# New planner costs and a new order for a two-layer attention and MLP kernel

## The chip, the cores and the metric

The kernel runs on one core of one Trainium2 chip. The metric is the device time of one launch in microseconds (us); three runs of the kernel before gave 1412.83 to 1413.08, with a median of 1412.99. The core has five engines that run side by side, each with its own in-order queue: TensorE (PE, matmuls into PSUM), ScalarE (ACT, exponentials and gelu), VectorE (DVE, elementwise work), GpSimd (POOL) and SyncE (SP, which issues DMAs). They wait for one another by semaphores.

## The reference

Four residual blocks: attention, MLP, attention, MLP, both layers with the same weights. S = 2048 rows, D = 512, H = 32 heads of 16 columns, F = 1792.

```python
def _A_ref(x, wqkv, wo):
    qkv = (x @ wqkv).reshape(B, S, 3, H, Dh).transpose(2, 0, 3, 1, 4)
    q, k, v = qkv[0], qkv[1], qkv[2]
    scores = einsum("bhqd,bhkd->bhqk", q, k) * (Dh ** -0.5)
    p = softmax(scores, axis=-1)
    o = einsum("bhqk,bhkd->bhqd", p, v)
    return o.transpose(0, 2, 1, 3).reshape(B, S, D) @ wo

def _B_ref(x, w1, b1, w2, b2):
    return einsum("bsf,fd->bsd", gelu(einsum("bsd,df->bsf", x, w1) + b1), w2) + b2

x = x + _A_ref(layernorm(x), A_wqkv, A_wo)
x = x + _B_ref(layernorm(x), B_w1, B_b1, B_w2, B_b2)
x = x + _A_ref(layernorm(x), A_wqkv, A_wo)
x = x + _B_ref(layernorm(x), B_w1, B_b1, B_w2, B_b2)
```

## The kernel before, in words

**Blocks.** The scores of the two layers are cut into 4096 blocks (called cells in the code) of 128 keys by 512 columns. A block is one matmul on 32 rows of the TensorE array (L1595), so up to four blocks, one for each row group `a` = 0 to 3, run side by side; each fills one PSUM bank. An exponential then turns scores into the weights of the softmax. Most blocks go to ACT: one ACTIVATE (L2245) takes two or three neighbouring banks at once. There are two slots of banks, (0, 1, 2) and (3, 4), and later bank 5 joins the second; while ACT works on one slot, PE fills the other. The other blocks go to DVE, which evicts a bank with one multiply and add into 16-bit integers that are the bits of a rough exponential (L1862, `dfirst`); POOL or DVE adds constants to make shifted copies (L2108 and L2110, `shift`, `dchain`), and their products with V and with three scaled copies of V (`vcopies`, L1523) are summed. So a block on ACT costs PE one product with V (L2312, `pvs`) and a block on DVE four. Four products run side by side in a round on 32 columns each.

**Passes.** `passes` cuts the work into 84 passes, each for one group of heads in one segment of query rows. The table KD lists for each kind of pass the key blocks that DVE may take: 1320 blocks in all. In the order that the kernel before issues, DVE takes 1236 of them. Counted by pass, the missing 84 are: 17 of 32 in the first eight passes, 36 of 160 in the next eight (these 16 are the first segment of layer 0), 4 in the rest of layer 0, 27 in the 25 passes of layer 1 that alternate between its first two segments, and none in the last 19 passes. A listed block that DVE doesn't take goes to ACT (`next_act`).

**Side work.** Layernorm, the projections, the output matrix, the two MLP matmuls and the gelu of other segments are spread between the exponentials. A gelu needs another activation table than the exponential, so each pair of gelu ACTIVATEs (L1273) has a table load before and after it. Where PE would idle long, the planner inserts matmuls whose result isn't used (`fill`, L1583).

**The planner.** The order of every engine's queue is written out when the kernel is built. `_Sched.run` keeps a clock for each engine, looks which operations are ready, and issues the one that can start first; `_ready` adds up when an operation's inputs are there (the end of what makes them, and LATENCY of its engine), `_cost` how long it takes. Priorities decide between operations that are ready, and an operation with a `slack` may be issued ahead of one that would end after it had to start. Before each score matmul, `attach`, `more`, `trade` and `swap` decide whether blocks for DVE, or a third block for ACT, go along: the bank must be free in the plan by the score's start (within TOL or SOFT), and DVE's clock must not be later than SWAP after it. `solo` issues a block for DVE alone when ACT's clock is far ahead of PE's. The costs never reach the chip; there only the order counts, and each engine goes on as soon as its semaphores allow.

The numbers in NAMES are settings of these decisions. ROWS holds sets of them and PIECES says which set is in force in each of 100 equal pieces of the 4096 blocks (`turn`, `take`).

Of the kernel before, what the change touches and what calls it, by code (L numbers as in the profile page):

```python
# [22 lines left out]
PVB = 6  # L23
# [71 lines left out]
         "ALONE", "AHEAD", "PSHIFT", "QUEUE", "SOLO", "BACK", "SIDE", "BOTH", "DMAX", "GMAX", "PMORE", "DUMORE", "GRACE", "PPS", "WAIT", "SOFT",  # L95
         "CLOSE",)
ROWS = (
# [42 lines left out]
)  # L140
PIECES = (5, 12, 11, 14, 27, 2, 39, 7, 26, 39, 20, 29, 23, 24, 15, 13, 24, 19, 11, 24, 24, 37, 25, 40, 37, 16, 30, 36, 38, 2, 21, 15, 39,
          24, 5, 14, 26, 38, 26, 37, 31, 9, 29, 3, 15, 17, 40, 26, 17, 28, 1, 19, 31, 31, 8, 29, 22, 20, 15, 39, 10, 21, 26, 37, 11, 9, 0,
          29, 29, 32, 36, 15, 33, 35, 21, 5, 34, 6, 26, 39, 41, 9, 17, 40, 18, 2, 31, 37, 27, 2, 29, 20, 36, 37, 39, 4, 12, 20, 39, 34)
CLOSE = 0.35
BOTH = 1
DMAX = 2
# [27 lines left out]
RWIDE = 2  # L174
AHEAD = 24
PSHIFT = 3
EXPC = 0.054
PFIX = 0.173
PWORD = 0.00164
VFIX = 0.151  # L180
# [147 lines left out]

OWN = 0.022
HEAD = 0.14  # L330
LATENCY = {"pe": 0.2175, "act": 0.21, "dve": 0.139, "pool": 0.153328, "sp": 0.1}
OVERLAP = 0.083
ROUND = 1.02
MROUND = 1.033


class _Sched:
# [130 lines left out]
    def _cost(self, op):  # L468
        if op.eng == "act" and op.writes[0][0] in "XKQ":
            return 0.48  # L470
        if op.eng == "dve":
            return max(op.cost - OVERLAP, 0.07)
        if op.eng == "pe":
            return op.cost * ((ROUND if op.writes[:1] == ["B.%d" % PVB] else MROUND) if op.mode == "P" else 1.0) + (SW if op.mode != self.mode else 0.0)
        return op.cost

    def active(self, t):
# [106 lines left out]
SW = 0.107  # L584
# [117 lines left out]
class _Plan:  # L702
# [558 lines left out]
    def gelu(self, l, seg):  # L1261
        T = self.T
        n = seg[2]
        for p in range(NFC // 2):
            yield ("need", ("h", l, seg, p))
        half = NFC // GP
# [2 lines left out]
            if n == 512:  # L1269
                g = g.rearrange("p a q -> p (a q)")  # L1270
            gk = self.gkeys(seg, range(f, f + half))
            yield _Op("act", 0.065 + 0.4267 * half * n / 512 + 1.31,
                      lambda e, g=g: e.activation(out=g, in_=g, func=ACT.Gelu_apprx_tanh), reads=gk, writes=gk, prio=2)  # L1273
            for p in range(f // 2, (f + half) // 2):
                yield ("give", ("g", l, seg, p))
# [352 lines left out]
    def turn(self):  # L1628
        self.piece += 1
        globals().update(zip(NAMES, ROWS[PIECES[self.piece]]))  # L1630

    def take(self, c):
        self.scored += 1
        self.left[c[0]] -= 1
        self.due[c[0]] += 1
        if self.piece + 1 < len(PIECES) and self.scored * len(PIECES) >= (self.piece + 1) * self.total:
            self.turn()
# [795 lines left out]
```

## Time and profile before

| what | value |
|---|---|
| median of three runs | 1412.99 us |
| profiled execution, its own time | 1412.66 us |
| profiled execution, span from the first to the last instruction | 1410.8 us |
| mean granted TensorE clock | 1.000 |
| PE busy | 1384.3 us |
| ACT busy | 1387.5 us |
| DVE busy | 1258.0 us |
| POOL busy | 983.4 us |

Busy is the time in which an engine has at least one instruction under way. A group row gives line, engine, operation, tile written and tiles read, the form and the count, then the busy time, the mean duration of one in ns, and the idle time before the group with what ended it. A row of one line's instructions has the shortest, median and longest duration in ns, the first and last start in us, and the most frequent forms of that tile. A timeline row has the start, the length from the first start to the last end, and the count of instructions that were merged; a piece of the chain has start, length and count. A row of a window has its length, then for PE, PE's weight loads, DVE, ACT and POOL the busy time and the count, then the granted clock and the DMA share with GB/s. A row of the waits has who waited for whom, the total in us, how often, and the longest.

### The profile page before, as it was taken

The numbers are of one execution on the slowest core, as the hardware profiler recorded it, in microseconds if no ns is written. First come the engines' busy times: TensorE is split into PE (matmuls) and PEld (weight loads), VectorE is DVE, ScalarE is ACT, GpSimd is POOL, SyncE is SP. The second block draws the span as 40 slices with busy tenths as digits, with TensorE's granted clock in tenths as the row PEclk, the third lists the DMA queues.
The fourth block names the chain that finished last, engine by engine and source line by source line (L and its number), as shares of the span: only waits on it lengthen the run. The fifth ranks groups of instructions, "written<-read, shape, count | busy, mean of one in ns | idle before, by whom it ended". The sixth has DMA issues, their size and how long they took to land.

```text
span 1410.8 us, 45496 instructions
## 1 busy us (share of the span) xinstructions
PE 1384.3 (98%) x19322; PEld 412.1 (29%) x19322; DVE 1258.0 (89%) x2482; ACT 1387.5 (98%) x1398; POOL 983.4 (70%) x1231
## 2 busy tenths in 40 slices
PE   9999999999999999999999999999999999999999
PEld 3222222222222222222222222222222222334346
DVE  8999999988998899988899898899988888999884
ACT  7999999999999999999999999999999999999995
POOL 1479787885877777756775669657876866877671
PEclk9999999999999999999999999999999999999999
DMA  5200000114221232212512241100114223201121
GB/s 148 68 2 2 2 2 18 38 47 128 69 55 31 62 113 69 54 46 86 119 36 50 62 117 58 46 17 17 32 57 116 63 62 117 74 17 40 29 59 55
DMA packets 122307, 80.39 MB, mean 57 GB/s; under 512 B 36732, under 2 KB 121084, under 8 KB 122108
## 3 DMA queue, kind: packets, MB, share of 16 engines
q1 hardware_dynamic: 122108, 77.49, 19.8%
q8 instruction: 155, 2.54, 0.7%
q14 instruction: 44, 0.36, 0.1%
HBM read 65.67 MB, written 4.19 MB: 50 GB/s over the span
## 4 chain that ended last, share of the span: by engine, by line
ACT 90%; PE 8%; DVE 1%; DMA 0%; issue 0%; DVEq 0%
ACT pt L2245 76%; ACT kt L2245 4%; PE ps L712 3%; ACT g L1273 3%; ACT q L2245 3%; ACT v L2245 2%; PE ps L2312 2%; PE ps L1595 2%; ACT L2245 1%; ACT L1273 1%; ACT g L2245 0%; DMA wr<-in_B_w_dram 0%; DVE kt L1862 0%; DVE dp L1862 0%; PE ps L899 0%; DVE stats L845 0%
## 5 line engine op out<-in xcount | busy, mean ns | idle before, releaser
L2245 ACT ACTIVATE pt<-ps 128x1024 bf16<-128x1024 f32 (+1 forms) x1181 | 1173.3, 1219 | 1.3 <-PE ps L1595 1.1
L2108 POOL INT64_ADD dp<-dp x739 | 598.8, 819 | 169.2 <-DVE dp L1862 35.9
L1595 PE MATMUL ps<-qp,kt 32*128 32x512 bf16 x4096 | 540.4, 384 | 12.7 <-ACT pt L2245 8.2
L1862 DVE TENSOR_SCALAR dp<-ps 128x512 uint16<-128x512 f32 x748 | 498.9, 682 | 49.2 <-PE ps L1595 44.3
L1595 PEld LDWEIGHTS ps<-qp,kt 32*128 32x128 bf16 x4096 | 136.0, 91 | 570.1 <-ACT pt L2245 460.4
L2312 PE MATMUL ps<-pt,v 128*17 128x512 bf16 (+1 forms) x2827 | 281.0, 359 | 1.6 <-DVE v L1004 0.7
L2312 PE MATMUL ps<-dp,vc 128*17 128x512 bf16 (+1 forms) x2532 | 279.9, 356 | 0.4 <-ACT pt L2245 0.2
L2108 POOL INT64_ADD kt<-kt x251 | 203.3, 815 | 95.3 <-DVE kt L1862 43.0
L1862 DVE TENSOR_SCALAR kt<-ps 128x512 uint16<-128x512 f32 x256 | 172.3, 683 | 21.5 <-PE ps L1595 19.6
L712 PE MATMUL ps<-xf,wr 128*32 128x512 bf16 (+1 forms) x1888 | 134.1, 365 | 0.0
L2108 POOL INT64_ADD v<-v x119 | 96.7, 817 | 52.4 <-DVE v L1862 16.4
L2312 PE MATMUL ps<-dp,v 128*17 128x512 bf16 (+1 forms) x844 | 123.7, 357 | 3.4 <-DVE xt L1073 2.8
L2312 PE MATMUL ps<-kt,vc 128*17 128x512 bf16 (+1 forms) x954 | 117.7, 339 | 0.9 <-POOL kt L2108 0.6
L712 PE MATMUL ps<-wr,g 128*32 128x512 bf16 x1408 | 106.0, 383 | 0.2 <-DMA wr<-in_B_w_dram 0.2
L2312 PEld LDWEIGHTS ps<-dp,vc 128*17 128x17 bf16 x2532 | 76.5, 89 | 60.5 <-issue 29.0
L1862 DVE TENSOR_SCALAR v<-ps 128x512 uint16<-128x512 f32 x120 | 81.3, 683 | 13.1 <-PE ps L1595 12.1
L2312 PEld LDWEIGHTS ps<-pt,v 128*17 128x17 bf16 x2827 | 70.2, 88 | 75.4 <-issue 54.2
L2108 POOL INT64_ADD xf<-xf x63 | 50.9, 808 | 58.4 <-DVE xf L1862 39.3
L1255 DVE TENSOR_SCALAR g<-ps,hb1t 128x512 bf16<-128x512 f32 (+1 forms) x112 | 78.9, 706 | 6.3 <-PE ps L712 6.2
L2312 PE MATMUL ps<-kt,v 128*17 128x512 bf16 (+1 forms) x449 | 73.8, 352 | 0.3 <-DVE xt L1073 0.2
L2245 ACT ACTIVATE kt<-ps 128x1024 bf16<-128x1024 f32 x64 | 69.0, 1189 | 0.0
L2312 PE MATMUL ps<-v,vc 128*17 128x512 bf16 x360 | 60.4, 381 | 0.1
(127 smaller groups left out, 1450.8 us busy)
## 6 DMA issues: line engine op xcount, KB each, us to landing
wr<-in_B_w_dram SPq DMA_DIRECT2D x174, 256.0 KB, 2.9
wr<-in_A_wqkv_dram SPq DMA_DIRECT2D x24, 256.0 KB, 3.1
x<-in_A_x_dram SPq DMA_DIRECT2D x7, 512.0 KB, 4.6
wr<-in_A_wo_dram SPq DMA_DIRECT2D x10, 256.0 KB, 4.0
kept<-x SPq DMA_DIRECT2D x4, 512.0 KB, 3.0
x<-kept SPq DMA_DIRECT2D x4, 512.0 KB, 3.9
out_dram<-x SPq DMA_DIRECT2D x16, 128.0 KB, 1.7
q<-in_B_w_dram SPq DMA_DIRECT2D x3, 512.0 KB, 5.6
```

The costliest lines, as they stand in the source:

```text
L712: return [lambda e, a=a: e.matmul(out[32 * a:32 * a + 32, :], lhsT=lhsT[:, 32 * a:32 * a + 32], rhs=rhs, start=start, stop=stop, tile_posi ...
L1255: yield _Op("dve", 0.21 + n / 966, lambda e, fc=fc, pb=pb: e.tensor_scalar(T["G"][:, fc, q], pb, T["HB1T"][:, fc:fc + 1], None, op0=ALU.ad ...
L1273: lambda e, g=g: e.activation(out=g, in_=g, func=ACT.Gelu_apprx_tanh), reads=gk, writes=gk, prio=2)
L1595: return (lambda e: e.matmul(o, lhsT=lhsT, rhs=rhs, start=True, stop=True, tile_position=(32 * a, 0)), ["K%d.%d.%d" % (l, gb, kt // 4), "Q ...
L1862: yield _Op("dve", 0.682, lambda e: e.tensor_scalar(u, self.bank(b), E_SCALE, E_BIAS, op0=ALU.mult, op1=ALU.add), reads=["B.%d" % b], writ ...
L2108: op = _Op("pool", PFIX + PWORD * 128 * n * (1 + both), lambda e: e.int64_add(dst, src, by * PACKED), reads=reads, writes=writes)
L2245: yield _Op("act", EXPC + 0.4267 * n, lambda e, src=src, dst=dst: e.activation(out=dst, in_=src, func=ACT.Exp, scale=0.25), reads=["B.%d" ...
L2312: op.fns.append(lambda e, o=o, lhsT=q[0][0][m], rhs=q[0][1][:, n * m:n * m + n], a=a, st=st, sp=sp: e.matmul(o, lhsT=lhsT, rhs=rhs, start= ...
```

## The change

Five numbers of the planner change, one is new, and two are merged:

```diff
-EXPC = 0.054
+EXPC = 0.0635
...
-LATENCY = {"pe": 0.2175, "act": 0.21, "dve": 0.139, "pool": 0.153328, "sp": 0.1}
+LATENCY = {"pe": 0.2175, "act": 0.17, "dve": 0.115, "pool": 0.153328, "sp": 0.1}
 OVERLAP = 0.083
-ROUND = 1.02
-MROUND = 1.033
+ROUND = 1.013
+INTO = 0.008
...
-            return op.cost * ((ROUND if op.writes[:1] == ["B.%d" % PVB] else MROUND) if op.mode == "P" else 1.0) + (SW if op.mode != self.mode else 0.0)
+            return op.cost * (ROUND if op.mode == "P" else 1.0) + (SW + (INTO if op.mode == "P" else 0.0) if op.mode != self.mode else 0.0)
...
-            yield _Op("act", 0.065 + 0.4267 * half * n / 512 + 1.31,
+            yield _Op("act", 0.065 + 0.4267 * half * n / 512 + 1.46,
```

An exponential over n banks costs EXPC + 0.4267 n in the plan. A round of four products or of side work costs `MM` (0.2132) times ROUND, and SW (0.107) is added where PE changes between score matmuls (mode S) and rounds (mode P); INTO comes on top where it changes into rounds.

ROWS has 39 sets in place of 42, and PIECES takes the 39 in a new sequence of 100. The first set and the pieces, before and after (the second number of a set is SLACK, the third LATE, the fifth OPENING):

```diff
-    (0.5, 0.3, 0.7, 0.2, 10, 10, 2, 6, 1, 1, 2, 2, 5, 0.3, 0.4, 2, 3.5, 24, 3, 4, 0.4, 1.0, 0, 1, 2, 3, 1, 2, 0.3, 2, 0.15, 0.0, 0.35,),
...
+    (0.5, 0.1, 0.7, 0.2, 18, 10, 2, 6, 1, 1, 2, 2, 5, 0.3, 0.4, 2, 3.5, 24, 3, 4, 0.4, 1.0, 0, 1, 2, 3, 1, 2, 0.3, 2, 0.15, 0.0, 0.35,),
+    (0.5, 0.3, 0.7, 0.2, 18, 10, 2, 6, 1, 1, 2, 2, 5, 0.3, 0.4, 2, 3.5, 24, 3, 4, 0.4, 1.0, 0, 1, 2, 3, 1, 2, 0.3, 2, 0.15, 0.0, 0.35,),
...
-PIECES = (5, 12, 11, 14, 27, 2, 39, 7, 26, 39, 20, 29, 23, 24, 15, 13, 24, 19, 11, 24, 24, 37, 25, 40, 37, 16, 30, 36, 38, 2, 21, 15, 39,
...
+PIECES = (20, 3, 16, 16, 17, 7, 3, 6, 20, 34, 1, 25, 25, 4, 29, 17, 24, 34, 36, 38, 37, 26, 16, 38, 34, 28, 32, 22, 4, 16, 4, 23, 4, 1, 0,
...
```

Nearly all sets before have SLACK 0.3 and most after have 0.2. Sets of before with MID (the fourteenth number) at 1.4 are gone. KD, the passes, the instructions and their forms are the same.

More of the change, by code (lines that the diff above doesn't have):

```diff
@@ L97 @@
 ROWS = (
[42 rows of a table removed]
-)
-PIECES = (5, 12, 11, 14, 27, 2, 39, 7, 26, 39, 20, 29, 23, 24, 15, 13, 24, 19, 11, 24, 24, 37, 25, 40, 37, 16, 30, 36, 38, 2, 21, 15, 39,
-          24, 5, 14, 26, 38, 26, 37, 31, 9, 29, 3, 15, 17, 40, 26, 17, 28, 1, 19, 31, 31, 8, 29, 22, 20, 15, 39, 10, 21, 26, 37, 11, 9, 0,
-          29, 29, 32, 36, 15, 33, 35, 21, 5, 34, 6, 26, 39, 41, 9, 17, 40, 18, 2, 31, 37, 27, 2, 29, 20, 36, 37, 39, 4, 12, 20, 39, 34)
[39 rows of a table added]
+)
+PIECES = (20, 3, 16, 16, 17, 7, 3, 6, 20, 34, 1, 25, 25, 4, 29, 17, 24, 34, 36, 38, 37, 26, 16, 38, 34, 28, 32, 22, 4, 16, 4, 23, 4, 1, 0,
+          16, 24, 20, 30, 8, 18, 33, 11, 19, 26, 19, 33, 16, 21, 9, 2, 29, 10, 32, 36, 35, 13, 12, 34, 28, 36, 5, 21, 19, 30, 11, 15, 16,
+          38, 25, 30, 5, 26, 24, 29, 3, 28, 16, 27, 23, 30, 0, 22, 15, 24, 23, 30, 21, 33, 11, 14, 24, 30, 10, 31, 16, 36, 38, 8, 4)
 CLOSE = 0.35
```

78 rows, old and new, of the table ROWS are left out of this document.

## The prediction

> **What bounds the kernel now.** I read the page first (busy shares, slices, chain), then one engine at a time: groups by line, single pieces of the chain, three windows, the waits. On the page:
>
> ```profile
> PE 1384.3 (98%) x19322; PEld 412.1 (29%) x19322; DVE 1258.0 (89%) x2482; ACT 1387.5 (98%) x1398; POOL 983.4 (70%) x1231
> ...
> DVE  8999999988998899988899898899988888999884
> ACT  7999999999999999999999999999999999999995
> ...
> PEclk9999999999999999999999999999999999999999
> ...
> ACT 90%; PE 8%; DVE 1%; DMA 0%; issue 0%; DVEq 0%
> ```
>
> Two engines are 98% busy, but the chain that ended last runs over ACT for 90%, and a matmul's recorded end contains its pipeline, so ACT is the candidate. ACT's records overlap too, so "busy" is no proof; the step from one exponential to the next is. Two pieces of the chain, both of exponentials two banks wide:
>
> ```profile
> 451.17 16.50 ACT pt L2245 x18
> 1308.66 6.42 ACT v L2245 x7
> ```
>
> 16.50 / 18 and 6.42 / 7 are both 0.917 us, though one record lasts longer:
>
> ```profile
> L2245 ACT ACTIVATE pt<-ps 128x1024 bf16<-128x1024 f32 x1011 | 970.8, 1158 | 0.2
> L2245 ACT ACTIVATE pt<-ps 128x1536 bf16<-128x1536 f32 x170 | 255.6, 1585 | 1.2 <-PE ps L1595 1.1
> ```
>
> The third bank adds 1585 - 1158 = 427 ns, the planner's 0.4267 a bank. So an exponential costs 0.4267 a bank plus 0.917 - 2 x 0.4267 = 0.0636 fixed: 0.917 for two banks, 1.344 for three. Now the number of each, by the exponentials (first five rows, grouped by the tile written) and the score blocks that VectorE turns into exponentials (last five):
>
> ```profile
> L1595 PE MATMUL ps<-qp,kt 32*128 32x512 bf16 x4096 | 540.4, 384 | 12.7 <-ACT pt L2245 8.2 <-ACT q L2245 0.6 <-ACT v L2245 0.3
> L2245 ACT ACTIVATE pt<-ps x1181: 1018/1178/1756, 12.2 to 1382.0; 128x1024 bf16<-128x1024 f32 x163, 128x1536 bf16<-128x1536 f32 x34
> L2245 ACT ACTIVATE kt<-ps x64: 1018/1179/1642, 200.7 to 836.9; 128x1024 bf16<-128x1024 f32 x61, 128x1536 bf16<-128x1536 f32 x3
> L2245 ACT ACTIVATE v<-ps x49: 1023/1182/1619, 1009.5 to 1380.7; 128x1024 bf16<-128x1024 f32 x43, 128x1536 bf16<-128x1536 f32 x6
> L2245 ACT ACTIVATE q<-ps x37: 1023/1196/1634, 209.0 to 1206.6; 128x1024 bf16<-128x1024 f32 x30, 128x1536 bf16<-128x1536 f32 x7
> L2245 ACT ACTIVATE g<-ps x5: 1024/1208/1720, 875.1 to 902.5; 128x1024 bf16<-128x1024 f32 x3, 128x1536 bf16<-128x1536 f32 x2
> L1862 DVE TENSOR_SCALAR dp<-ps x748: 624/682/693, 33.5 to 1376.8; 128x512 uint16<-128x512 f32 x187
> L1862 DVE TENSOR_SCALAR kt<-ps x256: 627/683/693, 152.5 to 1364.9; 128x512 uint16<-128x512 f32 x128
> L1862 DVE TENSOR_SCALAR v<-ps x120: 629/685/693, 199.9 to 668.0; 128x512 uint16<-128x512 f32 x120
> L1862 DVE TENSOR_SCALAR xf<-ps x64: 645/688/693, 30.4 to 1215.4; 128x512 uint16<-128x512 f32 x64
> L1862 DVE TENSOR_SCALAR xp<-ps x48: 645/682/693, 32.4 to 789.1; 128x512 uint16<-128x512 f32 x48
> ```
>
> Of 4096 blocks, 748 + 256 + 120 + 64 + 48 = 1236 go to VectorE, 2860 to ACT in 1181 + 64 + 49 + 37 + 5 = 1336 exponentials: 2860 - 2 x 1336 = 188 of three banks, 1148 of two. The gelus interrupt them:
>
> ```profile
> 307.27 2.13 ACT L2245 ACTIVATE pt<-ps 128x1024 bf16<-128x1024 f32 x2
> 309.42 1.28 ACT L1273 ACT_TABLE_LOAD   x1
> 310.71 6.27 ACT L1273 ACTIVATE g<-g 128x3584 bf16<-128x3584 bf16 x2
> 317.00 1.28 ACT L2245 ACT_TABLE_LOAD   x1
> 318.29 1.02 ACT L2245 ACTIVATE pt<-ps 128x1024 bf16<-128x1024 f32 x1
> ```
>
> From the end of one exponential (309.40) to that of the next (319.31), less its own 0.917, a gelu pair costs 9.0 us; seven lie between the first and the last exponential (14 of the wide gelus). The sum: 1148 x 0.917 + 188 x 1.344 + 7 x 9.0 = 1368.4, and three casts at the start of some 0.5 make 1369.9. The three windows, before, from first to last exponential, and after (columns PE, PEld, DVE, ACT, POOL):
>
> ```profile
> 0.00:12.23 12.23, 10.46 (x98) 4.63 (x98) 9.74 (x48) 4.89 (x11) 2.87 (x9) 1.00 0.85 250
> 12.23:1383.05 1370.82, 1348.96 (x18613) 391.24 (x18616) 1236.94 (x2394) 1370.16 (x1367) 980.53 (x1222) 1.00 0.20 55
> 1383.05:1410.80 27.75, 24.87 (x620) 16.20 (x612) 11.31 (x41) 12.44 (x21) 0.00 (x0) 1.00 0.17 50
> ```
>
> 1369.9 of 1370.8: ACT stalls for about 1 us in all. So the time is 12.2 (opening) + ACT's work + 27.8 (tail), and an order is worth what it takes off ACT: 2860 blocks x 0.4267 + exponentials x 0.0636. The profiled run took 1412.66 against a span of 1410.8 and a median of 1412.99; I work in the span and add 2.2.
>
> **The change part by part.** No instruction is edited; the planner's numbers and its table of settings change, and the order comes out new.
>
> *Exponential, 0.054 to 0.0635.* The trace says 0.0636. The plan's ACT gets 1336 x 0.0095 = 12.7 us longer, the chip's not at all. *Gelu, 1.31 to 1.46.* Two halves cost 2 x (0.065 + 2.987 + 1.46) = 9.02 in the plan against 9.0 traced (8.72 before): 7 x 0.3 = 2.1 us more plan time. So the plan sees 14.8 us of ACT time that it overlooked, and can fill it with work of the others.
>
> What can move is bounded: the lists KD offer 1320 blocks and 1236 are done, so 84 remain, 53 of them in the first segment's passes (17 in its first eight, 36 in the next eight), 4 later in layer 0 and 27 in the 25 passes of layer 1 in which two segments alternate. Where the list is used up, a slower plan of ACT moves no block. The first 16 passes and those 25 hold 512 + 832 of 4096 blocks, so 14.8 x 1344 / 4096 = 4.9 us of the overlooked time lies there. Back-to-back evictions start 0.60 apart:
>
> ```profile
> 700.04 0.67 DVE L1862 TENSOR_SCALAR kt<-ps 128x512 uint16<-128x512 f32 x1
> 700.64 0.68 DVE L1862 TENSOR_SCALAR dp<-ps 128x512 uint16<-128x512 f32 x1
> ...
> 700.81 0.61 POOL L2108 INT64_ADD kt<-kt  x1 [1.70 <-DVE kt L1862]
> ```
>
> so 4.9 / 0.6 = 8 blocks. Each saves half an exponential, 0.4585: **-3.7 us**. Bounds: all 84, -38.5; and below zero too, since nothing forces a new order to reach 1236: 12 lost (one for each of twelve passes short of blocks, an estimate from the counts above) is +5.5. I take 8 because the rate row is of the very instruction. The cover is VectorE, 1236.94 of 1370.82 busy, and POOL, 980.53; PE pays three more products a block, 3/4 of a 0.213 round, 8 x 0.16 = 1.3 us in its own slack. That slack shows in the waits of score matmuls for a bank, 0.42 each; they come back with more work ahead of them:
>
> ```profile
> PEld ps L1595 <- ACT pt L2245: 460.4, 1094, 1.3
> PEld ps L1595 <- DVE dp L1862: 12.1, 28, 0.5
> ```
>
> [...]
>
> *Releases: ACT 0.21 to 0.17, DVE 0.139 to 0.115.* The lone exponential above ended at 319.31, and the score that waited for it started at
>
> ```profile
> 319.37 0.10 PEld L1595 LDWEIGHTS ps<-qp,kt 32*128 32x128 bf16 x3 [0.55 <-ACT pt L2245]
> ```
>
> 0.06 later; its record outlasts the step by 1.02 - 0.917 = 0.10, so the plan should charge 0.16: 0.17 fits. For DVE the eviction at 700.04 ends 700.71 and POOL starts 0.10 later: 0.77 from its start, while the plan charges 0.599 + 0.115 = 0.714 (0.738 before). So the new figure lies 0.06 below this row, 0.024 further than the old. In an in-order queue that is a short wait, mostly on POOL (30% idle). I charge ACT +0.7 us of new stalls; bounds 0 and +3 (the 28 waits on an eviction above, grown by 0.1 each).
>
> *Single rounds (1.02 and 1.033 to 1.013, and 0.008 a switch).* A side round in its own visit goes from 0.2203 + 0.107 to 0.216 + 0.115, 0.004 dearer; a product pair 0.005 dearer, a side pair equal. Nothing on the chip: 0, with +-1 for what it reorders.
>
> *Settings and pieces.* Mostly SLACK 0.3 to 0.2. They choose how many exponentials get a third bank: 20 more of three banks drop 10 exponentials, 10 x 0.0636 = **-0.6** (bounds -3 and +3, some hundred either way, an estimate from the 188 there are). Opening: 0, with +-1 (its window has DMA busy for 0.85 of the time, and no load changes). Tail: the ending work is 24.87 of 27.75 us on PE, -0.4 with bounds -2 and +2.
>
> Sum: -3.7 - 0.6 - 0.4 + 0.7 = -4.0. Span 1406.8, time **1408.8** (1412.8 - 4.0, between the profiled run and the median). 0.2% is 2.8 us, about what a measurement here tells from no change.
>
> **The rivals.**
>
> *A: nothing to gain.* In three quarters of the passes the list is used up already, and ACT is back to back, so a truer plan has nothing to repair. Blocks within 6 of 1236: 1412.8 +- 2.8. For it: the missing 1 us of stalls. Against: 84 blocks left.
>
> *B: much more.* A third of the 84 is taken, 28 x 0.4585 = 12.8: 1400. For it: VectorE's idle 134 us in the middle window. Against: the passes short of blocks are the loaded ones (slices of DVE at 9 there).
>
> *C: slower, by lost blocks.* A score may take a VectorE block only if VectorE's plan is free within SWAP 0.5 of the score's start. ACT's release is 40 ns earlier in the plan, so the score starts earlier and VectorE looks 40 ns later; a chance missed costs 0.4585. From 7 lost blocks (3.2 us) it is slower; 14 lost, 1419.2. For it: the first segment's full VectorE. Against: 14.8 us more plan time.
>
> *D: slower, by starved exponentials.* DVE's releases are charged below the row by 0.06; each time PE's queue stands at a product whose block is late, the score behind is late. A score has 0.42 us to spare, so it decides only where three or four such errors add up; 4.7 us of stalls eat the gain, 7.5 make it slower; 70 of 0.15 are 10.5: 1412.8 - 4.7 + 10.5 = 1418.6. Against: 1 us of stalls now.
>
> **How the numbers follow.** Forecast band (-2.8 to -9, that is 1404 to 1410): 0.43. B (below 1404): 0.11. A: 0.21. C: 0.17. D: 0.08. Faster 0.43 + 0.11 = 0.54, same 0.21, slower 0.25. The range, 1402 to 1417, leaves out the far half of B and the far part of C; the likeliest case's own is 1404 to 1410.
>
> **What would show it.** The five counts of VectorE evictions sum to about 1244 (C: below 1230; B: above 1260). Exponentials sum to about 1322, some 208 of three banks. ACT's work by the two steps still accounts for the window from first to last exponential to within 2 us (D: not). Opening 12.2 and tail 27 to 28 us unchanged. I am wrong if the eviction count moves and the time does not follow at 0.4585 a block, or if the tail moves by more than 2 us.

## The result, and the profile after

| | before | after |
|---|---|---|
| median of seven runs, us | 1412.99 | 1417.24 |
| lowest to highest, us | 1412.68 to 1413.17 | 1414.65 to 1419.75 |
| profiled execution, span | 1410.8 | 1415.6 |
| mean granted TensorE clock | 1.000 (profiled execution) | 0.999 in three of seven, else 1.000 |

The ratio is 1.003 (95% interval 1.002 to 1.004): the kernel became slower by 0.3%, 4.25 us, where I had forecast 4.2 us less. It also scatters over 5 us in the seven runs, where the kernel before scatters over 0.5. (In the longer series of the experiments below, on three chips, the kernel before itself spreads over 1.8 to 2.8 us, in 15 to 27 runs each.) The profiled execution took 1417.74. Line numbers are three lower than before.

The page of the kernel after, the lines that answer to those of before:

```profile
PE 1379.4 (97%) x19360; PEld 413.4 (29%) x19360; DVE 1259.9 (89%) x2482; ACT 1388.1 (98%) x1377; POOL 994.3 (70%) x1247
...
DVE  8999999889998899988998789999978878999883
ACT  7999999999999999999999999999999999999995
...
PEclk9999999999999999999999999999999999999999
...
PE 56%; ACT 25%; DVE 15%; DMA 2%; POOL 1%; issue 1%; DVEq 0%
```

The busy shares hardly differ from those of before; ACT is again at 98%. The chain that ended last does: ACT carried 90% of it, and now carries 25%, with PE at 56% and DVE at 15%. The shares of the chain overstate what changed, since ACT still works for all but 10 us of the middle, as counted below; but other engines now make it wait at many places.

The counts, by the exponentials of each tile and the blocks that DVE evicts:

```profile
L2242 ACT ACTIVATE pt<-ps x1131: 1018/1081/1685, 12.2 to 1386.8; 128x1024 bf16<-128x1024 f32 x151, 128x1536 bf16<-128x1536 f32 x38
L2242 ACT ACTIVATE v<-ps x67: 1018/1045/1586, 991.4 to 1385.4; 128x1024 bf16<-128x1024 f32 x61, 128x1536 bf16<-128x1536 f32 x6
L2242 ACT ACTIVATE kt<-ps x64: 1018/1070/1557, 201.3 to 830.0; 128x1024 bf16<-128x1024 f32 x53, 128x1536 bf16<-128x1536 f32 x11
L2242 ACT ACTIVATE q<-ps x40: 1018/1079/1602, 224.5 to 1214.3; 128x1024 bf16<-128x1024 f32 x30, 128x1536 bf16<-128x1536 f32 x10
L2242 ACT ACTIVATE g<-ps x13: 1023/1472/1533, 351.5 to 902.8; 128x1536 bf16<-128x1536 f32 x7, 128x1024 bf16<-128x1024 f32 x6
...
L1859 DVE TENSOR_SCALAR dp<-ps x756: 625/680/693, 37.3 to 1381.8; 128x512 uint16<-128x512 f32 x189
L1859 DVE TENSOR_SCALAR kt<-ps x258: 628/682/693, 149.1 to 1373.8; 128x512 uint16<-128x512 f32 x129
L1859 DVE TENSOR_SCALAR v<-ps x110: 650/680/692, 198.5 to 650.5; 128x512 uint16<-128x512 f32 x110
L1859 DVE TENSOR_SCALAR xf<-ps x72: 650/683/692, 29.4 to 1221.7; 128x512 uint16<-128x512 f32 x72
L1859 DVE TENSOR_SCALAR xp<-ps x46: 629/680/692, 31.5 to 789.2; 128x512 uint16<-128x512 f32 x46
```

DVE takes 756 + 258 + 110 + 72 + 46 = 1242 blocks (1236 before), so ACT has 2854, in 1131 + 67 + 64 + 40 + 13 = 1315 exponentials: 2854 - 2 x 1315 = 224 of three banks and 1091 of two. ACT's work is 1091 x 0.917 + 224 x 1.344 + 63.0 for the gelus + 1.5 for the casts = 1366.0, 3.9 us less than before. The three windows:

```profile
0.00:12.23 12.23, 9.19 (x96) 4.26 (x96) 9.74 (x48) 4.89 (x11) 2.88 (x9) 1.00 0.84 248
12.23:1388.22 1375.99, 1346.78 (x18705) 394.23 (x18708) 1240.02 (x2397) 1370.89 (x1346) 991.41 (x1238) 1.00 0.20 56
1388.22:1415.60 27.38, 23.48 (x572) 14.92 (x560) 10.11 (x38) 12.33 (x20) 0.00 (x0) 1.00 0.10 32
```

The opening is the same 12.23, the tail 27.38 for 27.75. The middle holds 1375.99 us for 1366.0 of work: 10.0 us in which ACT stalls, where the kernel before has 1370.82 - 1369.9 = 0.9. So 1410.8 - 3.9 - 0.4 + 9.1 = 1415.6. Nearly all that was to be gained on ACT was gained, and stalls took it twice over.

From here on "stalls" is the sum over all steps from the end of one exponential to the end of the next, less the common step of its width (0.917 and 1.343 us), where that is over 0.012 us: 1.4 us in 16 places before, 10.5 us in 82 places after. The planner's own clock has 1.7 us of ACT idle in the order after and 2.6 in the order before. So before, the chip ran with fewer stalls than planned; after, it has 10.5 - 1.7 = 8.8 us more than its plan.

Some of them name their cause. The waits for DMA in the kernel after:

```profile
PEld ps L709 <- DMA wr<-in_B_w_dram: 4.1, 7, 1.7
PE ps L709 <- DMA wr<-in_B_w_dram: 2.2, 3, 1.4
DVE xln L1325 <- DMA xf<-xln: 1.3, 1, 1.3
DVE xln L873 <- DMA kt<-xln: 1.0, 1, 1.0
```

The second row lies within the first: where PE's weights are late (PEld), its matmuls (PE) are late at the same place. So PE stood for MLP weights for 4.1 us at 7 places; in the kernel before it was this:

```profile
PEld ps L712 <- DMA wr<-in_B_w_dram: 0.8, 2, 0.5
```

One of these stops in the chain (start, length, what), with the exponential behind it:

```profile
1049.38 0.01 PE ps L1592
1049.39 6.69 DMA wr<-in_B_w_dram
1056.08 0.04 issue
1056.12 0.61 PE ps L709 x8
...
1057.11 1.94 ACT L2242 ACTIVATE pt<-ps 128x1024 bf16<-128x1024 f32 x2 [1.13 <-PE ps L1592]
```

An MLP weight load issued at 1049.39 landed 6.69 us later, where the median of the 174 loads of that kind is 3.0. PE's queue stood at the side matmul that needs it, the score behind it was late, and ACT idled for 1.13 us.

### The profile page after: what moved, and what is told of

It reads as the page before. It is cut to its first block, busy times and chain, and to the rows that moved or that the text cites. A ratio compares the mean times of both kernels' runs of the same rounds, so it can differ in the third digit from the quotient of the medians.

```text
span 1415.6 us, 45592 instructions
## 1 busy us (share of the span) xinstructions
PE 1379.4 (97%) x19360; PEld 413.4 (29%) x19360; DVE 1259.9 (89%) x2482; ACT 1388.1 (98%) x1377; POOL 994.3 (70%) x1247
## 4 chain that ended last, share of the span: by engine, by line
PE 56%; ACT 25%; DVE 15%; DMA 2%; POOL 1%; issue 1%; DVEq 0%
ACT pt L2242 20%; PE ps L2309 19%; PE ps L1592 18%; PE ps L709 18%; DVE dp L1859 5%; DVE kt L1859 2%; DMA wr<-in_B_w_dram 1%; ACT v L2242 1%; ACT g L1270 1%; DVE stats L842 1%; ACT q L2242 1%; ACT g L2242 1%; ACT kt L2242 1%; DVE xln L873 1%; POOL dp L2105 1%
## 5 line engine op out<-in xcount | busy, mean ns | idle before, releaser
L2242 ACT ACTIVATE pt<-ps 128x1024 bf16<-128x1024 f32 (+1 forms) x1131 | 1133.5, 1151 | 4.2 <-PE ps L1592 3.3
L2105 POOL INT64_ADD dp<-dp x752 | 607.6, 818 | 167.4 <-DVE dp L1859 39.5
L2105 POOL INT64_ADD kt<-kt x257 | 207.8, 814 | 97.2 <-DVE kt L1859 45.5
L2309 PE MATMUL ps<-pt,v 128*17 128x512 bf16 (+1 forms) x2739 | 266.5, 359 | 1.8 <-POOL kt L2105 0.5
L2309 PE MATMUL ps<-kt,vc 128*17 128x512 bf16 (+1 forms) x960 | 123.1, 339 | 0.7 <-POOL kt L2105 0.4
L2105 POOL INT64_ADD v<-v x110 | 89.7, 821 | 44.7 <-DVE v L1859 19.5
L1859 DVE TENSOR_SCALAR v<-ps 128x512 uint16<-128x512 f32 x110 | 73.7, 681 | 9.0 <-PE ps L1592 8.4
L2242 ACT ACTIVATE kt<-ps 128x1024 bf16<-128x1024 f32 (+1 forms) x64 | 68.5, 1150 | 0.3 <-PE ps L1592 0.2
L2242 ACT ACTIVATE v<-ps 128x1024 bf16<-128x1024 f32 (+1 forms) x67 | 67.2, 1091 | 0.1
```

What stands on the lines that cost most here:

```text
L1859: yield _Op("dve", 0.682, lambda e: e.tensor_scalar(u, self.bank(b), E_SCALE, E_BIAS, op0=ALU.mult, op1=ALU.add), reads=["B.%d" % b], writ ...
L2105: op = _Op("pool", PFIX + PWORD * 128 * n * (1 + both), lambda e: e.int64_add(dst, src, by * PACKED), reads=reads, writes=writes)
L2242: yield _Op("act", EXPC + 0.4267 * n, lambda e, src=src, dst=dst: e.activation(out=dst, in_=src, func=ACT.Exp, scale=0.25), reads=["B.%d" ...
L2309: op.fns.append(lambda e, o=o, lhsT=q[0][0][m], rhs=q[0][1][:, n * m:n * m + n], a=a, st=st, sp=sp: e.matmul(o, lhsT=lhsT, rhs=rhs, start= ...
```

## The experiments

Two theories of the stalls stood at the start. R, the reserve (T in two of the texts below): the old costs had ACT 9.5 ns faster at each exponential than it is, so on the chip ACT fell behind its plan all the time, and whatever came late on PE, DVE, POOL or DMA was made up while it did; the new costs are true, and that reserve is gone. Its rivals: the new releases are too short, or this one order is unlucky. All differences below are between the median of an experiment and that of the kernel before on the same chip.

| run | to before, us | ratio (95%) | stalls, us (places) | runs with clock 0.999 |
|---|---|---|---|---|
| after | +4.25 | 1.003 (1.002 to 1.004) | 10.5 (82) | 3 of 7 |
| new tables, old costs | +31.4 | 1.0223 (1.0204 to 1.0241) | 16.3 (44) | 1 of 2 |
| new costs, old tables | +20.4 | 1.0144 (1.0126 to 1.0163) | 14.7 (69) | 0 of 2 |
| after, small weight loads | +2.21 | 1.0018 (1.0009 to 1.0027) | 7.5 (77) | 5 of 11 |
| the same and three rounds | +1.46 | 1.0009 (1.0001 to 1.0018) | 7.7 (77) | 0 of 11 |
| small loads, small POOL | -0.70 | 0.9996 (0.9986 to 1.0006) | 5.0 (46) | 2 of 8 |
| small loads, small side steps | -1.81 | 0.9988 (0.9978 to 0.9998) | 3.6 (38) | 2 of 8 |
| all four | -2.89 | 0.9978 (0.9968 to 0.9987) | 3.2 (29) | 0 of 9 |
| after, three rounds alone | +2.49 | 1.0017 (1.0007 to 1.0026) | 10.7 (89) | 0 of 10 |
| before, narrow exponentials | -9.78 | 0.9929 (0.9914 to 0.9944) | 6.3 (74) | 0 of 4 |
| before, small side steps | -0.90 | 0.9993 (0.9983 to 1.0003) | 0.7 (9) | 0 of 10 |

**One half of the change alone.** Old costs with the new sets and pieces, and new costs with the old ones (shortened):

```diff
 # e2: the kernel after
-EXPC = 0.0635
+EXPC = 0.054
 # e3: the kernel before
-EXPC = 0.054
+EXPC = 0.0635
 # and LATENCY, ROUND, MROUND / INTO and gelu likewise
```

> The old costs with the new tables of settings. The plan then has 1200 blocks on DVE and 1067 + 254 exponentials, so ACT's work is 14 us longer than before the change, and the plan itself leaves ACT idle for 15 us: about 1436 us by both theories. Theory T (the true costs took away a hidden reserve): unplanned stalls of ACT 1 to 3 us, as before the change. Rival O (this is chance, of one order): 4 to 8 us.

> The new costs with the old tables. The plan has 1218 blocks on DVE, 1131 + 205 exponentials and 10 us of planned idle time of ACT: 1430 us where nothing unplanned comes on top. Theory T (reserve gone): unplanned stalls 6 to 10 us, so 1436 to 1440 us. Rival O (chance of one order): 1 to 4 us, 1431 to 1434 us.

Measured: 1444.71 and 1433.63. Both are far slower than either kernel, with 1200 and 1218 blocks for DVE. Of their stalls the planner's clock has 14.9 and 10.1 us itself. What is not in the plan is 16.3 - 14.9 = 1.4 and 14.7 - 10.1 = 4.6 us by the sums, and 4.2 and about 5 us when it is counted place by place, since some planned stalls don't occur on the chip. For the old costs the first count fits theory T (1 to 3) and the second its rival (4 to 8). For the new costs both counts lie between the two bands, below the 6 to 10 of theory T and above the 1 to 4 of its rival, and the time of 1433.63 is one that the rival had forecast (1431 to 1434). So this pair doesn't decide between the theories, and T missed on the new costs. What it shows is that with either half alone the order gets far worse, so the change can't be priced by undoing a half of it; from here on I kept the orders and changed the work.

The first of them held something else. Windows of 3.4 us in the execution of the old costs with the new tables, with the granted clock third from last:

```profile
487.70:491.10 3.40, 3.16 (x57) 1.29 (x56) 1.90 (x4) 3.38 (x2) 0.91 (x2) 1.00 0.20 41
491.10:494.53 3.43, 1.85 (x30) 0.54 (x26) 1.14 (x2) 3.42 (x4) 0.00 (x0) 1.00 0.87 258
494.53:497.94 3.41, 3.41 (x30) 0.47 (x22) 2.69 (x6) 2.70 (x4) 0.61 (x1) 0.50 0.02 7
497.94:501.35 3.41, 3.41 (x48) 0.95 (x48) 3.09 (x7) 3.25 (x4) 1.41 (x2) 1.00 0.33 86
```

PE waits for most of 491.10 to 494.53; for the next 3.41 us the clock is at half, and ACT, busy before, is busy for 2.70 of 3.41. Counted by the starts of the matmuls (0.213 us for each, the planner's figure, side by side counted once; in this trace seven rounds in a row last 1.69 us and one 0.39, so they follow one another after 0.217), the array works 0.39 of 491.2 to 494.6. In the kernel after, the sparsest such stretch, 0.35, starts at 932.0; in the kernel before it is 0.52. The stretch ahead of the half clock still holds 30 matmuls, and PE's longest wait in it was 1.58 us. That the sparse stretch brought the half clock was my reading of this one place; how sparse the array must be for that, and for how long, was not shown.

**Loads that come in time.** The kernel after, each load of a weight ring slot 32 partitions high instead of 128 from the slot's second use on (the edit is shortened); the order is the same on all engines:

```diff
 def wload(self, piece, src, n, uses, w, over):
-    dst = self.T["WR"][w].rearrange("p (c f) -> p c f", c=n)
+    n = slice(0, 32) if w in self.whole else slice(0, 128)
+    dst, src = dst[n], src[n]
```

> The order of the kernel after on every engine, but from the second use of a buffer on, the ring's weight loads fetch 32 of 128 partitions (a quarter of the bytes; the rest of each weight tile is stale, so those matmuls compute something else in the same time). Theory L (late loads): the stalls of ACT behind a late load vanish, 1.24 + 0.35 + 0.27 us at 1057, 673 and 1171 us and, as the queues are emptier, the 1.09 us at 1085 us behind a late transposing load; with the short stalls that follow them 3 to 3.5 us, so about 1414 us, and the runs, which spread over 5 us after the change, lie within 1 us of each other. The 45 short stalls (about 5 us) stay. Rival S (loads are not the point): 1416 to 1418 us with the same spread.

Measured: 1415.49 (1414.67 to 1416.83). PE waits for no weight load any more, the stalls fall from 10.5 to 7.5 us, the time by 2.0 us against before. The time lies between the 1414 of theory L and the 1416 to 1418 of its rival, and the spread did not close to 1 us: the six runs with a mean clock of 1.000 took 1414.67 to 1415.49, the five with 0.999 took 1415.99 to 1416.83, 1.3 us more in the mean. So late loads are a part, and a lower clock in some of the runs is another.

**The half-clock stretch.** The same, and three rounds of zeros for PE at 931.2 us, where the array is sparse (the edit, shortened):

```diff
 # pvs, build: behind the one step planned at 926.86
+for x in range(3): for a in open columns:
+    e.matmul(bank(PVB)[32*a:32*a+17], lhsT=ZERO[:, 0:17], rhs=B2row, start=False, stop=False)
```

> The kernel after with its short weight loads (as in the run of small weights: ring loads of 32 partitions, so the weights are not the reference's), and three more rounds of TensorE, 12 matmuls of zeros added to the bank of the weighted sums, in the idle 0.8 us behind one step at 931.2 us of the span. Nothing else differs. There the array was busy 0.36 of its sparsest stretch of 3.41 us; with the 0.64 us of the three rounds it is 0.55, which is above the kernel before's lowest, 0.52. Theory W (the window at 931 us is what sets the clock to half for a stretch in 5 of 11 runs of that kernel, and 1.3 us is what it costs): every run has a mean clock of 1.000, times from 1414.6 to 1415.6, median 1414.9. Rival (half-clock stretches come from elsewhere or by chance): again 4 to 6 of 11 runs at 0.999 and times up to 1416.8, median 1415.5.

Measured: 1414.44 (1414.11 to 1414.95), 1.000 in all eleven. Theory W holds: with 0.64 us of matmuls that compute nothing (three rounds at 0.213; PE busy 2.44 us for 1.82 in the windows below), no run has a lower clock any more; of the 16 runs of the next two experiments, without the rounds and on the same chip, 4 have it. The window from 932.0 in the kernel after, and in this one:

```profile
932.00:935.40 3.40, 1.82 (x22) 0.49 (x19) 3.27 (x7) 3.40 (x4) 2.42 (x4) 1.00 0.00 0
```

```profile
932.00:935.40 3.40, 2.44 (x36) 0.67 (x30) 3.27 (x7) 3.40 (x4) 2.39 (x4) 1.00 0.00 0
```

Both of these executions kept the full clock (the 1.00), so a sparse stretch doesn't always lower it; that it does so here in the runs with 0.999 is inferred from their going away with the rounds.

The kernel after with nothing but these rounds leaves nothing out:

> The kernel after, whole, and the three rounds of zeros at 931 us alone (nothing is left out; zeros are added to sums). Theory W (half of the executions lose 1.3 us there): the median falls from 1417.24 to 1416.0 to 1416.7 and the lowest stays at 1414.5 to 1415; what is left of the spread, some 2 to 3 us, is that of the late loads. If the late loads trip the clock as well (the sparsest stretch at 1054 us is busy 0.41), some runs still show 0.999. Rival (the half-clock stretch is hidden where loads are late): 1417.2 as before, spread 4 to 5 us.

Measured: 1.0017 of before, 1416.68 (1415.40 to 1418.59), all ten at 1.000. The lower clocks are gone; a spread of 3.2 us stays, and with it the late loads. On this chip the kernel before spreads over 2.8 us in its 25 runs, so most of that spread need not come from the change. In this execution PE waits longest for a load at 674.3, 492.7 and 1188.6 us (1.5, 1.4 and 0.9 us), in the kernel after at 1056.1, 1170.3 and 671.9 (1.7, 0.8 and 0.6 us): one order is hit at other places, and by other amounts, from one execution to the next. That is how a scatter like this can come about, and with the small loads and the rounds the runs lie within 0.8 and 1.1 us (eleven and nine runs); that the late loads are all of it was not shown.

**DVE and POOL.** With the small loads, POOL's additions on a quarter of their words; and with the small loads, four kinds of DVE's side steps on a quarter of their columns (shortened; most of it from 300 us on, as the texts below say):

```diff
 # e6, shift, on POOL
-e.int64_add(dst, src, by * PACKED)
+e.int64_add(dst[..., 0:k // 4], src[..., 0:k // 4], by * PACKED)
 # e7, apply, and the products, scaled values and padded queries alike
-T["XLN"][:, x, :], T["X"][:, t % XT, :]
+T["XLN"][:, x, 0:128], T["X"][:, t % XT, 0:128]
```

> The kernel after with the short weight loads, and POOL's additions on a quarter of their words after the first 300 us, where they work in place or on the planes of their own (the rest of the words is left as it is, so the products are not the reference's). Order kept on all engines. Theory P (the stalls that are left once the loads come in time, 7.4 us in the profiled run, come from POOL: its results late, and DVE's steps on SBUF stretched where the two overlap, such as the products at line 1079 with 469 ns instead of 432): the stalls fall to 2 to 4 us and the time to 1409.5 to 1411.5. Rival (they come from DVE's own side steps or from PE): 6.5 to 8 us, 1414 to 1415.5.

> The kernel after with the short weight loads, and four kinds of DVE's side steps on a quarter of their columns (products at line 1079, normalized rows at line 873, scaled values at line 1520, padded queries at line 1539; after the first 300 us or from the second use of a buffer on; what they leave out is stale). Order kept on all engines; some 50 us of DVE's work go. Theory D (the stalls that are left come from DVE's side steps that run longer than planned and push the blocks and the results behind them): the stalls fall from 7.4 us to 2 to 3 us and the time to 1409.5 to 1411. Rival (PE's own rounds and changes of form are later than planned, so PE brings the scores late whatever DVE does): 5.5 to 8 us, 1413 to 1415.

Measured: 1412.28 with 5.0 us of stalls, and 1411.17 with 3.6 us. The first lies between theory P and its rival; the second just beyond the 2 to 3 us of theory D and well short of its rival. So of the 7.5 us some half goes with shorter side steps on DVE and a third with shorter additions on POOL. That is where these stalls can be taken off; which step was late isn't shown, since DVE's busy time in the middle also falls, from 1240.9 to 1213.2 us with the small side steps and to 1227.3 with the small POOL. How POOL weighs on DVE, the products at line 1079 show (shortest, median and longest in ns) from 320 us on, in the kernel after and with the small POOL:

```profile
L1079 DVE TENSOR_TENSOR ott<-xt,rc x58: 269/414/1257, 341.2 to 1391.0; 128x256 bf16<-128x256 f32 x42, 128x128 bf16<-128x128 f32 x16
```

```profile
L1079 DVE TENSOR_TENSOR ott<-xt,rc x58: 274/415/576, 341.1 to 1385.5; 128x256 bf16<-128x256 f32 x42, 128x128 bf16<-128x128 f32 x16
```

The median is the same; the longest falls from 1257 to 576 ns. The longest of the kernel after started 0.33 us into one of POOL's additions and ended some 0.3 us behind it (start, length, what):

```profile
340.89 1.30 POOL L2105 INT64_ADD v<-v  x1
341.22 1.26 DVE L1079 TENSOR_TENSOR ott<-xt,rc 128x256 bf16<-128x256 f32 x1
```

Of these 58 products of the kernel after, 38 overlap none of POOL's additions and take 269 to 426 ns; the 20 that overlap one take 273 to 1257. What holds such a product up was not shown. The planner keeps such steps apart, but on its own clock. The kernel before has such products too (from 320 us on, 38 without an overlap with 269 to 426 ns, 20 with one with 277 to 1069), so the overlap as such is not new.

All of it at once:

> The kernel after with all four things taken away at once: short weight loads, the three rounds of zeros at 931 us, POOL's additions and DVE's side steps on a quarter (as in the runs before; outputs are not the reference's). Theory (late loads, DVE's and POOL's side steps and the half-clock stretch are together what the forecast lacked): the stalls are the plan's own 1.7 us and at most 1 us more, the time 1409.2 to 1410.0 with every clock at 1.000, which is the 1408.8 that was predicted and 0.4 to 1.2 us. Rival (PE's own rounds are late by themselves): stalls as with the small side steps, 3.4 to 3.8 us, and 1410.8 to 1411.2.

Measured: 0.9978 of before, that is 2.89 us less, 3.2 us of stalls, every clock at 1.000. The forecast was 4.2 less. The middle window of this kernel:

```profile
12.23:1380.98 1368.75, 1345.39 (x18717) 393.29 (x18720) 1201.38 (x2397) 1367.49 (x1346) 596.43 (x1238) 1.00 0.10 26
```

1368.75 - 1366.0 = 2.8 of the 10.0 us are left. The 1411.3 lies above both bands that I wrote down, since this chip is 1.2 us slower with the kernel before as well; the 3.2 us of stalls lie nearer to the rival's 3.4 to 3.8 than to the 1.7 to 2.7 of the theory. 1.7 are the plan's own and 1.5 stay unexplained.

**Was it a reserve?** Here the kernel before is put to the test, in its own order. First ACT is brought to the pace that the old costs believed in (shortened):

```diff
 # exps
-src, dst = bank(...), self.unit(run)
+src, dst = src[:, :, 0:506], dst[:, :, 0:506]     # 512 at the first use of a buffer
```

> The kernel before, its order kept on every engine, its exponentials 506 columns a bank wide where they were 512 (from the second use of a buffer on, so the last 6 columns of each are stale). By the step from 1024 to 1536 columns, 0.834 ns a column, a two-bank exponential falls by 10.0 ns and a three-bank one by 15.0 ns: 1148 x 10.0 + 188 x 15.0 = 14.3 us less work on ACT, about the 9.5 ns each by which the old costs had ACT faster than it is. Theory R (the too fast ACT of the old costs was a reserve: whatever came late on PE, DVE or POOL was made up while ACT lagged behind its plan): with ACT at the plan's pace the stalls between exponentials go from 1.4 us to 8 to 11 us, and the time is 1413.0 - 14.3 + 7 to 9.5 = 1406 to 1408. Rival L (the old releases, longer by 0.04 to 0.06 us, were the reserve, and they still stand in this order): the stalls are the plan's own 2.6 us and some more, 3 to 4 us, and the time is 1400 to 1401.

Measured: 1403.20 (1402.28 to 1404.66). The steps fell from 916.6 to 906.6 and from 1343.2 to 1328.4 ns: 1120 x 10.0 + 177 x 14.8 = 13.8 us less work (39 exponentials kept their width). The span fell by 1410.8 - 1402.1 = 8.7. The rest went into stalls: 6.3 us in 74 places, for 1.4 in 16. PE now waits longer for loads that were not changed:

```profile
PEld ps L712 <- DMA wr<-in_B_w_dram: 2.8, 4, 1.2
```

That is 2.8 us for 0.8 before, and the chain goes over to the others:

```profile
ACT 52%; PE 36%; DVE 9%; DMA 1%; POOL 1%; issue 1%; POOLq 0%
```

So there was a reserve, and it hid 4.9 us in that order by the profiled execution (13.8 - 9.8 = 4.0 by the medians); I had expected 7 to 9.5 by R and at most 2.6 by the rival, and it is between. Second, the side steps of the kernel before on a quarter of their columns:

> The kernel before, its order kept, DVE's four kinds of side steps on a quarter of their columns as in the run on the kernel after (outputs are not the reference's; the weight loads are whole). Theory R (before, ACT lags behind its plan by 9.5 ns at each exponential, and this hides what is late on DVE): nothing to gain, stalls 1.0 to 1.4 us for 1.4, and 1412.4 to 1413.0. Rival (late side steps cost any order the same): it gains what the kernel after gained, 3.3 us, 1409.7; there are only 1.4 us of stalls in the profile to be gained, so 1411.6 is the least that it can give.

Measured: 0.9993 of before (0.9983 to 1.0003). The same edit that takes 3.9 us of stalls off the kernel after (7.5 to 3.6) takes 0.7 off the kernel before, for there are no more than 1.4. This fits the reserve, by which late side steps cost nothing as long as ACT is later still; with so little to be gained, it can't show it by itself.

## Why the prediction was wrong

One row of the kernel after belongs beside the steps below, the waits of score matmuls for ACT (460.4 us in 1094 waits before):

```profile
PEld ps L1592 <- ACT pt L2242: 425.0, 1007, 1.6
```

- **What bounds it** was right for before (ACT back to back; PE's 98% is made of matmul records of 0.38 us in rounds that follow one another after 0.22). I took from it that the ACT time which the plan had overlooked was free to be filled. It was not free: in part it was what the other engines lived on (4.9 us of it, by the narrow exponentials). Of "the plan's ACT gets 12.7 us longer, the chip's not at all", the first half means that the plan now packs PE, DVE, POOL and the loads against the true ACT, with no margin.
- **Eight more blocks, -3.7, and twenty more of three banks, -0.6**: six more and 36 more, ACT's work -3.9 for -4.3. That the sum comes so near is in part luck, as one count fell short and the other went over; no run tests the rate of 0.6 us a block or the 4.9 us of overlooked time where blocks were left.
- **Opening 0, tail -0.4**: 12.23 to 12.23, 27.75 to 27.38. Right.
- **New stalls on ACT +0.7, bounds 0 and +3**: this step failed. It is +9.1 us by the windows. I had bounded it by one wait only, scores behind an eviction, and had let the 0.42 us that a score waits for its bank stand for slack everywhere. Those waits are 0.42 us each in the kernel after too (the row above), though 1007 for 1094: the mean says nothing of the places where PE comes late. Against before, the ladder gives 4.25 - 2.21 = 2.0 us for late loads, 2.21 - 1.46 = 0.75 for the half-clock stretch and 1.46 + 2.89 = 4.35 for DVE's and POOL's side steps, 7.1 of the 8.4 us between forecast and result. The first two steps are hardly larger than the intervals or smaller (some 1.3 us to either side of each median); the third is clear of them. They rest on the stalls of the profiled executions (10.5, 7.5, 3.2) and on the clocks.
- **"Against: 1 us of stalls now"**, with which I put rival D at 0.08, was the error in the weights. D is what came: 70 stalls of 0.15 were written down, 82 of 0.13 measured, 1418.6 against 1417.24, and the sign that I had set for D, a window that ACT's work leaves open by more than 2 us, showed with 10.0. But the small number of stalls before was no sign of engines in time, as the narrow exponentials show: at the plan's pace the same order has 6.3. D's own cause, the DVE release 0.06 below its row, was not shown: no run changed the releases alone. So that its numbers fit is partly luck.
- **A, B, C.** A's count came, 1242 being within 6 of 1236, but not its time, 1412.8 +- 2.8. B and C did not come: blocks rose by 6, not by 28, and none were lost on balance.
- **A single time.** I gave the kernel after the scatter of the kernel before. Part of its 5 us goes with a clock that I had no term for. The row PEclk of the page doesn't show it: this execution kept the full clock, and 3.41 us at half would hardly count in a slice of 35 us. (The sum also has a slip of 0.2: 1406.8 + 2.2 is 1409.0, not 1408.8.)

What stays open: which of the five numbers spent the reserve (exponential, gelu or the releases), since each moves the order; how much of the 9.1 us belongs to this one order, beyond the 4.9 that the order before had hidden, as no second order by the new costs with its own tables was run; and 1.5 us of stalls that are left when loads, clock and side steps are all eased.

## What to carry to other kernels

A planner that charges its bottleneck engine too little can give the other engines slack on the chip, as here; before the charge is corrected, look at what arrives late without being seen, by the rows of the waits and by shrinking the bottleneck's work in the same order. An engine at 98% busy with almost no stalls shows that the others are in time at its present pace, not at a faster one. When a kernel's runs scatter more after a change, list the granted clock and the late loads of each execution, and measure the kernel before as often.

## What I had not expected of the hardware

- In the run of the new tables with the old costs, the clock fell to half for 3.41 us behind a stretch of 3.4 us in which the array worked 0.39 of the time; in the kernel after (0.35 in its sparsest stretch) and three variants that keep its order, 12 of 34 runs show a mean clock below 1.000, and in the three kernels with the added rounds none of 30; nor does any of the 67 runs of the kernel before (0.52) beside the experiments. In the three variants the runs with the lower clock took 1.0 to 1.5 us longer in the mean.
- The same kind of 256 KB load lands after 3.0 us in the median (the 174 MLP weight loads of the kernel after). Behind the opening the slowest took 6.9 us there. PE waited for such loads for 4.1 us at 7 places, and in the same order with the three rounds for 5.8 us at 8, the longest at other loads.
- Between two chips the kernel before differs by 1.2 us (1412.98 and 1414.19), which is why only ratios on one chip are compared here.
